# Cached attention on one core: the query weights of rounds 1 to 3 are loaded two head pairs at a time

## The chip, the core and the metric

The kernel runs on one core of a Trainium2 chip. TensorE multiplies matrices and writes to PSUM, eight banks of 2 KB a partition; VectorE and ScalarE copy out of PSUM and do the softmax; SyncE (SP) issues every load and store, which 16 DMA engines carry out; GpSimd does almost nothing here. The metric is the device time of one execution in microseconds. Three runs of the kernel before took 440.2, 445.95 and 443.5 us, so its median is 443.5 us.

## The reference: attention over a cache, with both projections

```python
B, Sq, D = 8, 112, 640
H, Sk, Dh = 32, 512, 192
q = (x @ wq).reshape(B, Sq, H, Dh).transpose(0, 2, 1, 3)
scores = einsum("bhqd,bhkd->bhqk", q, k_cache) * Dh ** -0.5
p = softmax(scores)
o = einsum("bhqk,bhkd->bhqd", p, v_cache)
out = o.transpose(0, 2, 1, 3).reshape(B, Sq, H * Dh) @ wo
```

All tensors are bf16. K and V have 8 x 32 x 512 x 192 elements each; wq is 640 x 6144, wo 6144 x 640.

## The kernel before

**Tiling.** The 32 heads go in four rounds of eight. In a round r, the kernel goes through the eight batches, and for each batch through two quads of four heads: 64 steps n in all, numbered in that order, two steps to a pair of round and batch i = n // 2. The queries of a round are made in two groups g = 2r and 2r + 1, four batches (448 rows) each. A group has four head pairs lp, and a head pair has 384 columns of wq, three blocks c of 128. So a fill Q(g, lp, c) is five matmuls over D = 640, each 128 weights by 448 rows, and evQ copies it out of PSUM.

**A step.** Sm and St make the scores of a step (with qc, copies of queries to the other half of the partitions, ahead of them); smax on VectorE scales them and takes the maximum, exp on ScalarE, rc and norm on VectorE divide by the sum; PT transposes p on TensorE and evPT copies it out; PVt and PVm multiply with V; evPV copies the result to oT. O multiplies oT with wo, and oacc adds that up over the rounds. For steps 57 to 61, p is transposed by a DMA (TD) instead of PT. exp of step n + 2 writes where p of step n lay, so it waits for PT or TD of step n.

**Loads.** K of a round and batch comes by a transposing DMA, (K, i), or plain, in halves of four heads, (KN, i, ...), and is then transposed on TensorE (KT). V comes in halves (V, i, half) of 768 KB. x comes in three loads X and is transposed on TensorE in seven chunks XT(c) of 128 rows, which evX copies out of PSUM.

**Query weights.** One SBUF tile wq_sb holds the weights of one round, four head pairs. (WQ, r, lp, n) loads n head pairs from lp on, 640 rows of n x 768 B (line 205): with n = 1 it is 480 KB, with n = 2, 960 KB. It overwrites weights of the round before, so for r > 0 it waits for all the fills of group 2r - 1 that read them, three for each head pair (line 207). Fills of the round wait for the load that brings their head pair (wq_piece, line 697). Each load has the semaphore of its first head pair.

**What sets the order.** Nothing is reordered at run time. ORDER_PE, ORDER_ACT, ORDER_DVE and ORDER_SP list the operations of each engine by hand; BANKS says which PSUM bank each result gets. An engine goes through its list, and for each operation waits for the semaphores of what it needs (lines 37 to 48); what stands behind a waiting operation waits too. An operation that writes a bank waits for the copies out of what lay in it before. On SP there is one rule more (lines 1105 to 1108): each load waits for an earlier load to land, the nearest one that has loads of a total size of at least 0.95 between it and this one. Sizes are in units of 1.5 MB: a V half is 0.5, a K of the transposing kind counts 1.5, a WQ load 1/3 for each head pair.

```python
            add("SP", ("WQ", r, lp, n), [q_done(2 * r - 1, lp + i, c) for i in range(n) for c in range(3)] if r else [],
                emit, f"mWQ{lp}", 16)
```

In round 0, head pairs 1 and 0 come as single loads and pairs 2 and 3 as one; in rounds 1 to 3 all four come one by one. Of the fills that they wait for, TensorE's list has Q(1, 1, 2) behind PT(2) and KT(3, 0); Q(1, 3, 0) behind KT(4, 0); Q(3, 1, 1) behind PT(19) and Q(3, 3, 2); Q(3, 3, 1) between the two halves of O(1, 4); Q(5, 1, 2) ahead of the scores of step 37, and Q(5, 3, 1) behind PT(37). Q(4, 0, 0), the first reader of round 2's weights, follows Q(3, 1, 1) with Q(3, 2, 2), PVt(18) and both PVm(18) between them.

**The start.** TensorE runs 18 matmuls on zeros, then XT 0, 1, 3, 2, then Q(0, 1, 1) and Q(0, 0, 0). XT(1) and XT(3) both have bank 4, so XT(3) waits for evX(1). evX 0, 3 and 2 are ScalarE's, evX 1 is VectorE's. Q(0, ...) reads all four chunks.

Of the kernel before, what the change touches and what calls it, by code (L numbers as in the profile page):

```python
# [52 lines left out]
def build_mha_kernel(nc, x, k_cache, v_cache, wq, wo, out):  # L53
# [33 lines left out]
    with ExitStack() as es:  # L87
# [145 lines left out]
        def pv_all(n):  # L233
# [108 lines left out]
            ('evX', 0), ('evX', 3), ('evX', 2), ('evQ', 0, 0, 0), ('evQ', 0, 0, 1), ('evK', 0, 1, 1), ('evK', 0, 1, 0),  # L342
# [73 lines left out]
            ('evX', 1), ('evQ', 0, 1, 1), ('evQ', 0, 1, 0), ('evK', 0, 0, 0), ('evX', 5), ('evK', 0, 0, 1), ('qc', 0),  # L416
            ('evQ', 0, 3, 1), ('smax', 0, 0), ('evK', 0, 3, 0), ('smax', 0, 1), ('smax', 0, 2), ('smax', 0, 3),
# [783 lines left out]
```

## Time and profile before

| | before |
|---|---|
| median of three runs | 443.5 us (440.2 to 445.95) |
| the profiled execution | 439.52 us |
| its span, first to last instruction | 437.5 us |
| TensorE busy (matmuls) | 420.4 us, 96% |
| VectorE busy | 375.2 us, 86% |
| ScalarE busy | 337.5 us, 77% |
| mean granted TensorE clock | 0.994 |
| bytes moved by DMA | 122.03 MB, mean 279 GB/s |
| loads of wq | 14 of 480 KB, median 6.2 us from issue to landing; 1 of 960 KB, 7.5 us |

The profile is of one execution. Its rows give a start in us from the beginning of the span, a duration, the engine (PE is TensorE, DVE VectorE, ACT ScalarE; SPq is SyncE's sequencer), the line of the kernel, the operation, what is written and read, and the number of instructions merged in the row; in square brackets the idle time of the engine before it and what ended it. On SPq, start and duration are those of the issue, not of the transfer; rows of the DMA view give KB and the us from an issue to its landing. The chain of waits is followed back from the last instruction; its rows have start, duration and what ran or was awaited. In the view by windows a row has the stretch and its length, then for PE, PEld, DVE, ACT and POOL the busy us and the number of instructions, then the granted clock, the share of the DMA engines that were busy, and GB/s.

### The profile page before, as it was taken

To read this page: it belongs to the slowest core of one execution; us is meant where nothing else is said; L and a number is where in the kernel's file an instruction comes from. 1 tells how busy PE (TensorE), PEld (TensorE's weight loads), DVE (VectorE), ACT (ScalarE), POOL (GpSimd) and SP (SyncE) were. 2 spreads that over 40 slices of the span, in tenths; PEclk is the share of its full clock that TensorE was granted. 3 is DMA by queue.
4 is the path that set the end of the run, shared out by engine and by line. 5 is a ranking of instruction groups with operands and counts; after the bars stand their busy time and mean duration, and the time that the engine had idled before them with its cause. 6 is when DMAs were issued, how large, how long until landed. Compare 5 with 4: busy or idle time off the path is not lost.

```text
span 437.5 us, 16223 instructions
## 1 busy us (share of the span) xinstructions
PE 420.4 (96%) x6805; PEld 290.6 (66%) x6805; DVE 375.2 (86%) x1198; ACT 337.5 (77%) x741; POOL 0.7 (0%) x6
## 2 busy tenths in 40 slices
PE   7999999899999999989999999999999999998986
PEld 4566667676766767657676666676667667665886
DVE  1399999889898899979899889989989889997971
ACT  3499999897978786778787668877878777866764
POOL 0000000000000000000000000000000000000000
PEclk9999999999999999999999999999999999999999
DMA  8999999999999999999999999999999999999963
GB/s 272 369 348 340 345 236 320 194 331 356 234 293 261 306 231 364 346 204 303 225 215 342 302 212 274 361 368 244 233 252 347 228 246 367 285 253 238 227 189 95
DMA packets 222857, 122.03 MB, mean 279 GB/s; under 512 B 165312, under 2 KB 222784, under 8 KB 222784
## 3 DMA queue, kind: packets, MB, share of 16 engines
q1 hardware_dynamic: 222784, 120.99, 109.7%
q8 instruction: 54, 0.88, 0.8%
q14 instruction: 19, 0.16, 0.1%
HBM read 78.22 MB, written 1.15 MB: 181 GB/s over the span
## 4 chain that ended last, share of the span: by engine, by line
PE 76%; DMA 10%; ACT 8%; DVE 4%; issue 2%; SPq 0%; ACTq 0%; DVEq 0%
PE ps L939 18%; PE ps L719 16%; PE ps L772 16%; PE ps L917 10%; PE ps L905 6%; PE ps L873 5%; ACT p_sb L834 4%; DMA vt<-in_v_cache_dram 3%; DMA kt<-in_k_cache_dram 2%; DVE s_sb L829 2%; ACT kt L146 2%; ACT qr L146 1%; DMA wq_sb<-in_wq_dram 1%; DMA qr<-p_sb 1%; PE ps L671 1%
## 5 line engine op out<-in xcount | busy, mean ns | idle before, releaser
L834 ACT ACTIVATE p_sb<-s_sb,nmx 112x512 bf16<-112x512 f32 x256 | 182.9, 718 | 43.9 <-DVE s_sb L829 38.9
L829 DVE TENSOR_SCALAR_CACHE_REDUCE s_sb<-ps 112x512 f32<-112x512 f32 x256 | 168.6, 684 | 19.1 <-PE ps L772 10.2
L719 PE MATMUL ps<-xT_sb,wq_sb 128*128 128x448 bf16 x480 | 103.1, 358 | 2.5 <-ACT xT_sb L146 1.2
L772 PE MATMUL ps<-kt,qr 128*128 128x256 bf16 (+1 forms) x512 | 95.0, 272 | 1.7 <-DVE s_sb L829 1.7
L939 PE MATMUL ps<-oT_sb,wo_sb 128*128 128x448 bf16 (+1 forms) x480 | 92.8, 341 | 0.0
L772 PE MATMUL ps<-kt,qh 128*128 128x256 bf16 (+1 forms) x512 | 87.8, 272 | 0.0
L838 DVE TENSOR_SCALAR p_sb<-p_sb,rinv 112x512 bf16<-112x512 bf16 x256 | 81.3, 347 | 1.4
L719 PEld LDWEIGHTS ps<-xT_sb,wq_sb 128*128 128x128 bf16 x480 | 43.1, 98 | 41.5 <-issue 4.1
L939 PEld LDWEIGHTS ps<-oT_sb,wo_sb 128*128 128x128 bf16 x480 | 44.5, 98 | 34.6 <-issue 0.6
L146 ACT ACTIVATE oT_sb<-ps 128x672 bf16<-128x672 f32 x64 | 46.4, 726 | 25.1 <-PE ps L917 24.7
L146 ACT ACTIVATE pT_sb<-ps 128x768 bf16<-128x768 bf16 (+1 forms) x58 | 51.9, 901 | 11.2 <-PE ps L873 10.9
L772 PEld LDWEIGHTS ps<-kt,qr 128*128 128x128 bf16 (+1 forms) x512 | 44.1, 96 | 22.0 <-issue 11.2
L917 PE MATMUL ps<-pT_sb,vt 128*128 128x112 bf16 x944 | 55.7, 213 | 0.7 <-issue 0.7
L917 PEld LDWEIGHTS ps<-pT_sb,vt 128*128 128x128 bf16 x944 | 47.8, 98 | 5.3 <-issue 0.8
L834 ACT ACTIVATION_READ_ACCUMULATOR p_sb<-s_sb,nmx 112x1 f32 x256 | 49.5, 193 | 0.0
L772 PEld LDWEIGHTS ps<-kt,qh 128*128 128x128 bf16 (+1 forms) x512 | 44.1, 96 | 6.4
L147 DVE COPY pT_sb<-ps 128x1024 bf16<-128x1024 bf16 (+1 forms) x60 | 36.8, 621 | 5.2 <-PE ps L873 5.1
L146 ACT ACTIVATE qr<-ps 128x448 bf16<-128x448 f32 x65 | 34.2, 538 | 8.1 <-PE ps L719 7.5
L873 PE MATMUL ps<-ident,p_sb 64*128 64x64 bf16 (+1 forms) x1888 | 37.3, 185 | 2.1 <-issue 1.7
L873 PEld LDWEIGHTS ps<-ident,p_sb 64*128 64x128 bf16 (+1 forms) x1888 | 33.2, 94 | 8.3 <-issue 3.4
L905 PE MATMUL ps<-pT_sb,vt 128*64 128x112 bf16 x944 | 33.0, 215 | 2.6 <-DMA vt<-in_v_cache_dram 1.4
L905 PEld LDWEIGHTS ps<-pT_sb,vt 128*64 128x64 bf16 x944 | 25.6, 109 | 13.2 <-issue 2.6
(56 smaller groups left out, 248.6 us busy)
## 6 DMA issues: line engine op xcount, KB each, us to landing
vt<-in_v_cache_dram SPq DMA_DIRECT2D x64, 768.0 KB, 6.8
wo_sb<-in_wo_dram SPq DMA_DIRECT2D x8, 960.0 KB, 7.6
wq_sb<-in_wq_dram SPq DMA_DIRECT2D x14, 480.0 KB, 6.2
wo_sb<-in_k_cache_dram SPq DMA_DIRECT2D x6, 768.0 KB, 6.8
accT<-in_k_cache_dram SPq DMA_DIRECT2D x4, 768.0 KB, 6.9
vt<-in_k_cache_dram SPq DMA_DIRECT2D x2, 768.0 KB, 8.2
kt<-in_k_cache_dram SPq DMA_DIRECT2D x2, 768.0 KB, 6.5
out_dram<-xT_sb SPq DMA_DIRECT2D x8, 140.0 KB, 2.5
```

The source lines that it names most:

```text
L146: return e.activation(dst, src, ACTF.Copy)
L147: return e.tensor_copy(dst, src)
L671: ends = [e.transpose(psb[:, bank + t, y * 64:(y + 1) * 64], kn[i][64 * t:64 * t + 64, 2 * p + u, c * 128:(c + 1) * 128], ident[64 * t:64 ...
L719: mm = e.matmul(ps[:, bank, 0:SG], w, v, start=(dc == 0), stop=(dc == DC - 1))
L772: return e.matmul(ps[:, 2 * j + odd, hs], q, ktb[j][lo:hi, :, blk, h * 128:(h + 1) * 128], start=first, stop=last, skip_group_check=True)
L829: return e.tensor_scalar(s_sb[:, a, :].rearrange("p (e c) -> p e c", e=2), ps[0:SQ, 2 * j:2 * j + 2, h * 256:(h + 1) * 256], -scale, None, ...
L834: return e.activation(p_sb[:, k, :], s_sb[:, a, :], ACTF.Exp, bias=nmx[:, k:k + 1], scale=-1.0, accum_out=rsum[:, k:k + 1])
L838: return e.tensor_scalar(p_sb[:, k, :], p_sb[:, k, :], rinv[:, k:k + 1], None, op0=ALU.mult)
L873: ends.append(e.transpose(psb[:, bank + t, i * w:(i + 1) * w], p_sb[lo:hi, (4 * n + k) % 8, q * 128:(q + 1) * 128], ident[lo:hi, lo:hi]))
L905: mm = e.matmul(ps[64 * h:64 * h + 64, b0 + j, SQ:2 * SQ], vtb[:, h0 + 2 * j + h, d0:d0 + 64], pT(j, h, q), start=(q == 0), stop=(q == 3))
L917: mm = e.matmul(ps[:, b0 + j, 2 * h * SQ:(2 * h + 1) * SQ], vtb[:, h0 + 2 * j + h, d0:d0 + 128], pT(j, h, q), start=(q == 0), stop=(q == 3))
L939: mm = e.matmul(ps[:, bank_of["O", g, m], 0:nc_], wo_sb[:, k, m * 128:(m + 1) * 128], oT_sb[:, g % 2, k, 0:nc_], start=(k == 0), stop=(k = ...
```

## The change

In rounds 1 to 3 the four single loads of wq become two loads of two head pairs, (WQ, r, 0, 2) and (WQ, r, 2, 2), whose runs are 1536 B instead of 768 B. Their places in SP's list change too: in round 1 they stand where head pairs 1 and 3 were; in round 2 the first moves from ahead of K 12 to ahead of K 13, the second stands between the halves of V 12; in round 3 the first stands behind K 22 and the second between the halves of V 19. The order of all other loads among themselves stays, and TensorE's list stays as it is. The rule of lines 1105 to 1108 counts two thirds for a double, so some loads near them wait for another load's landing than before.

In the transposes of x, XT(3) has bank 2 in place of bank 4, and evX(2) moves from ScalarE's list to VectorE's, behind evX(1).

```diff
--- before.py
+++ after.py
@@ -339,7 +339,7 @@
             ('OF', 4), ('O6', 0, 1), ('PVm', 62, 0), ('PVm', 62, 1), ('O6', 2, 1), ('PVm', 63, 0), ('PVm', 63, 1),
             ('OF', 5), ('OL', 0, 0), ('OL', 1, 0), ('OL', 0, 1), ('OL', 1, 1), ('OF', 6), ('OF', 7)]
         ORDER_ACT = [
-            ('evX', 0), ('evX', 3), ('evX', 2), ('evQ', 0, 0, 0), ('evQ', 0, 0, 1), ('evK', 0, 1, 1), ('evK', 0, 1, 0),
+            ('evX', 0), ('evX', 3), ('evQ', 0, 0, 0), ('evQ', 0, 0, 1), ('evK', 0, 1, 1), ('evK', 0, 1, 0),
             ('evQ', 0, 1, 2), ('evQ', 0, 0, 2), ('evX', 6), ('evX', 4), ('evQ', 0, 3, 0), ('exp', 0, 0), ('evQ', 0, 3, 2),
             ('evQ', 0, 2, 1), ('evK', 0, 2, 1), ('evK', 1, 1, 1), ('exp', 0, 3), ('evK', 1, 2, 1), ('evQ', 0, 2, 2),
             ('exp', 0, 1), ('evK', 2, 1, 1), ('exp', 0, 2), ('evK', 1, 3, 0), ('evK', 1, 3, 1), ('evQ', 1, 1, 0),
@@ -413,8 +413,8 @@
             ('exp', 63, 0), ('exp', 63, 1), ('exp', 63, 2), ('evPV', 61), ('exp', 63, 3), ('evPT', 63, 1), ('oout', 3),
             ('evPV', 62), ('evPV', 63), ('oout', 5), ('oout', 4), ('oout', 6), ('oout', 7)]
         ORDER_DVE = [
-            ('evX', 1), ('evQ', 0, 1, 1), ('evQ', 0, 1, 0), ('evK', 0, 0, 0), ('evX', 5), ('evK', 0, 0, 1), ('qc', 0),
-            ('evQ', 0, 3, 1), ('smax', 0, 0), ('evK', 0, 3, 0), ('smax', 0, 1), ('smax', 0, 2), ('smax', 0, 3),
+            ('evX', 1), ('evX', 2), ('evQ', 0, 1, 1), ('evQ', 0, 1, 0), ('evK', 0, 0, 0), ('evX', 5), ('evK', 0, 0, 1),
+            ('qc', 0), ('evQ', 0, 3, 1), ('smax', 0, 0), ('evK', 0, 3, 0), ('smax', 0, 1), ('smax', 0, 2), ('smax', 0, 3),
             ('evK', 0, 2, 0), ('evK', 0, 3, 1), ('evK', 1, 1, 0), ('evK', 1, 2, 0), ('evQ', 0, 2, 0), ('qc', 2), ('qc', 1),
             ('evK', 2, 1, 0), ('rc', 0, 0), ('evQ', 1, 0, 1), ('rc', 0, 1), ('smax', 1, 0), ('smax', 1, 1), ('norm', 0, 1),
             ('evK', 1, 0, 1), ('evK', 1, 0, 0), ('norm', 0, 0), ('evK', 2, 2, 1), ('smax', 1, 2), ('smax', 1, 3),
@@ -554,25 +554,24 @@
         ORDER_SP = [
             ('X', 0), ('X', 1), ('WQ', 0, 1, 1), ('WQ', 0, 0, 1), ('KN', 0, 0, 4), ('X', 2), ('WQ', 0, 2, 2),
             ('KN', 0, 4, 4), ('KN', 1, 0, 4), ('KN', 1, 4, 4), ('KN', 2, 0, 4), ('KN', 2, 4, 4), ('V', 2, 0), ('V', 2, 1),
-            ('V', 0, 0), ('V', 0, 1), ('KN', 3, 0, 4), ('WQ', 1, 0, 1), ('KN', 3, 4, 4), ('KN', 4, 0, 4), ('KN', 4, 4, 4),
-            ('V', 1, 0), ('V', 1, 1), ('V', 3, 0), ('V', 3, 1), ('WQ', 1, 1, 1), ('KN', 5, 0, 4), ('K', 6), ('WQ', 1, 3, 1),
-            ('KN', 5, 4, 4), ('WQ', 1, 2, 1), ('V', 4, 0), ('V', 4, 1), ('K', 7), ('K', 8), ('WO', 0, 1), ('WO', 0, 0),
-            ('V', 6, 0), ('V', 5, 0), ('V', 6, 1), ('V', 5, 1), ('V', 7, 1), ('V', 7, 0), ('K', 10), ('K', 9), ('V', 8, 1),
-            ('V', 8, 0), ('K', 11), ('V', 9, 1), ('V', 9, 0), ('WQ', 2, 0, 1), ('K', 12), ('V', 10, 1), ('V', 10, 0),
-            ('V', 11, 0), ('K', 13), ('V', 11, 1), ('KN', 14, 4, 4), ('KN', 14, 0, 4), ('WQ', 2, 1, 1), ('WQ', 2, 2, 1),
-            ('V', 12, 1), ('V', 12, 0), ('WO', 1, 0), ('WO', 1, 1), ('WQ', 2, 3, 1), ('V', 13, 1), ('K', 16), ('K', 15),
-            ('V', 14, 0), ('V', 14, 1), ('V', 13, 0), ('V', 15, 1), ('K', 17), ('K', 18), ('K', 19), ('V', 15, 0),
-            ('V', 16, 0), ('V', 16, 1), ('V', 17, 0), ('V', 17, 1), ('V', 18, 0), ('V', 18, 1), ('K', 21), ('K', 20),
-            ('K', 22), ('WQ', 3, 1, 1), ('WQ', 3, 0, 1), ('V', 20, 0), ('WQ', 3, 2, 1), ('V', 20, 1), ('V', 19, 0),
-            ('V', 19, 1), ('WQ', 3, 3, 1), ('WO', 2, 0), ('WO', 2, 1), ('V', 21, 0), ('V', 21, 1), ('V', 22, 0),
-            ('V', 22, 1), ('K', 23), ('K', 25), ('K', 24), ('K', 26), ('V', 24, 0), ('V', 24, 1), ('V', 23, 0),
-            ('V', 23, 1), ('V', 25, 0), ('V', 25, 1), ('K', 28), ('K', 27), ('K', 29), ('V', 27, 0), ('V', 27, 1),
-            ('V', 26, 0), ('V', 26, 1), ('WO', 3, 0), ('WO', 3, 1), ('V', 28, 0), ('V', 28, 1), ('K', 30), ('K', 31),
-            ('TD', 57), ('TD', 58), ('V', 29, 0), ('V', 29, 1), ('TD', 59), ('V', 30, 0), ('TD', 60), ('V', 30, 1),
-            ('TD', 61), ('V', 31, 1), ('OUT', 1), ('V', 31, 0), ('OUT', 3), ('OUT', 2), ('OUT', 0), ('OUT', 5), ('OUT', 4),
-            ('OUT', 6), ('OUT', 7)]
+            ('V', 0, 0), ('V', 0, 1), ('KN', 3, 0, 4), ('KN', 3, 4, 4), ('KN', 4, 0, 4), ('KN', 4, 4, 4), ('V', 1, 0),
+            ('V', 1, 1), ('V', 3, 0), ('V', 3, 1), ('WQ', 1, 0, 2), ('KN', 5, 0, 4), ('K', 6), ('WQ', 1, 2, 2),
+            ('KN', 5, 4, 4), ('V', 4, 0), ('V', 4, 1), ('K', 7), ('K', 8), ('WO', 0, 1), ('WO', 0, 0), ('V', 6, 0),
+            ('V', 5, 0), ('V', 6, 1), ('V', 5, 1), ('V', 7, 1), ('V', 7, 0), ('K', 10), ('K', 9), ('V', 8, 1), ('V', 8, 0),
+            ('K', 11), ('V', 9, 1), ('V', 9, 0), ('K', 12), ('V', 10, 1), ('V', 10, 0), ('V', 11, 0), ('WQ', 2, 0, 2),
+            ('K', 13), ('V', 11, 1), ('KN', 14, 4, 4), ('KN', 14, 0, 4), ('V', 12, 1), ('WQ', 2, 2, 2), ('V', 12, 0),
+            ('WO', 1, 0), ('WO', 1, 1), ('V', 13, 1), ('K', 16), ('K', 15), ('V', 14, 0), ('V', 14, 1), ('V', 13, 0),
+            ('V', 15, 1), ('K', 17), ('K', 18), ('K', 19), ('V', 15, 0), ('V', 16, 0), ('V', 16, 1), ('V', 17, 0),
+            ('V', 17, 1), ('V', 18, 0), ('V', 18, 1), ('K', 21), ('K', 20), ('K', 22), ('WQ', 3, 0, 2), ('V', 20, 0),
+            ('V', 20, 1), ('V', 19, 0), ('WQ', 3, 2, 2), ('V', 19, 1), ('WO', 2, 0), ('WO', 2, 1), ('V', 21, 0),
+            ('V', 21, 1), ('V', 22, 0), ('V', 22, 1), ('K', 23), ('K', 25), ('K', 24), ('K', 26), ('V', 24, 0),
+            ('V', 24, 1), ('V', 23, 0), ('V', 23, 1), ('V', 25, 0), ('V', 25, 1), ('K', 28), ('K', 27), ('K', 29),
+            ('V', 27, 0), ('V', 27, 1), ('V', 26, 0), ('V', 26, 1), ('WO', 3, 0), ('WO', 3, 1), ('V', 28, 0), ('V', 28, 1),
+            ('K', 30), ('K', 31), ('TD', 57), ('TD', 58), ('V', 29, 0), ('V', 29, 1), ('TD', 59), ('V', 30, 0), ('TD', 60),
+            ('V', 30, 1), ('TD', 61), ('V', 31, 1), ('OUT', 1), ('V', 31, 0), ('OUT', 3), ('OUT', 2), ('OUT', 0),
+            ('OUT', 5), ('OUT', 4), ('OUT', 6), ('OUT', 7)]
         BANKS = [
-            (('XT', 0), 5), (('XT', 1), 4), (('XT', 3), 4), (('XT', 2), 7), (('Q', 0, 1, 1), 6), (('Q', 0, 0, 0), 4),
+            (('XT', 0), 5), (('XT', 1), 4), (('XT', 3), 2), (('XT', 2), 7), (('Q', 0, 1, 1), 6), (('Q', 0, 0, 0), 4),
             (('Q', 0, 0, 1), 1), (('Q', 0, 1, 0), 7), (('KT', 0, 0), 0), (('KT', 0, 1), 5), (('Q', 0, 1, 2), 7),
             (('XT', 4), 2), (('Q', 0, 0, 2), 3), (('XT', 5), 6), (('XT', 6), 7), (('Q', 0, 3, 2), 6), (('Q', 0, 3, 1), 6),
             (('KT', 0, 3), 4), (('Q', 0, 3, 0), 4), (('Q', 0, 2, 0), 4), (('Q', 0, 2, 1), 4), (('KT', 0, 2), 0),
```

## The prediction, made before the change was run

> **What bounds the kernel now.** I read the page's busy shares first, then the order of time on SP (the engine that issues every load), then the times to landing, then the waits of TensorE.
>
> ```profile
> PE 420.4 (96%) x6805; PEld 290.6 (66%) x6805; DVE 375.2 (86%) x1198; ACT 337.5 (77%) x741; POOL 0.7 (0%) x6
> ...
> DMA  8999999999999999999999999999999999999963
> ```
>
> Two resources are full at once: TensorE (96%) and the DMA engines (90% or more in every slice from the second to the 38th). So a change that saves DMA time pays only where TensorE waits for a load, and one that stops TensorE or lets the DMA queue run dry can cost at once. TensorE's waits that end with a load or with what a load holds up are few; here they are, from the order of time on PE and ACT:
>
> ```profile
> 209.79 0.58 PE L905 MATMUL ps<-pT_sb,vt 128*64 128x112 bf16 x16 [0.69 <-DMA vt<-in_v_cache_dram]
> 284.43 0.58 PE L905 MATMUL ps<-pT_sb,vt 128*64 128x112 bf16 x16 [0.75 <-DMA vt<-in_v_cache_dram]
> 398.72 0.28 PE L772 MATMUL ps<-kt,qr 128*128 128x256 bf16 x1 [1.70 <-DVE s_sb L829]
> 397.12 0.72 ACT L834 ACTIVATE p_sb<-s_sb,nmx 112x512 bf16<-112x512 f32 x1 [2.03 <-DMA wq_sb<-p_sb]
> ```
>
> The last two belong together: the exponentials of step 59 wait 2.03 us for the DMA transpose of step 57 (its landing frees their place in p_sb), and through VectorE's maximum TensorE waits 1.70 us. That transpose stands in SP's queue behind the last two K transposes; the first row is SP's order of time, the second the chain of waits:
>
> ```profile
> 376.87 15.08 SPq L158 DMA_TRANSPOSE kt<-in_k_cache_dram  x2
> 392.05 4.99 DMA wq_sb<-p_sb
> ```
>
> SP is done with the K transposes at 376.87 + 15.08 = 391.95 and issues the transpose of p at 392.05. So the end is set by how far SP's queue has come at 392 us, and by TensorE where it is later than that. Those are the two delays that I follow.
>
> **The change part by part.** First the price of a load. A load's landing is its issue plus its time to landing, and in a full queue a load costs the time from the landing before it to its own. The rows are SP's order of time and, from the DMA view of short windows, the time to landing of the load issued there (the row with 6.34 is from the chain of waits, which has both in one):
>
> ```profile
> 4.60 0.37 SPq L179 DMA_DIRECT2D accT<-in_x_dram  x1
> 7.49 0.37 SPq L205 DMA_DIRECT2D wq_sb<-in_wq_dram  x1
> accT<-in_x_dram SPq DMA_DIRECT2D x1, 480.0 KB, 7.7
> wq_sb<-in_wq_dram SPq DMA_DIRECT2D x1, 960.0 KB, 7.5
> 268.67 0.53 SPq L167 DMA_DIRECT2D vt<-in_v_cache_dram  x1
> vt<-in_v_cache_dram SPq DMA_DIRECT2D x1, 768.0 KB, 7.3
> 271.11 6.34 DMA wq_sb<-in_wq_dram
> 55.13 8.05 SPq L158 DMA_TRANSPOSE kt<-in_k_cache_dram  x1
> kt<-in_k_cache_dram SPq DMA_TRANSPOSE x1, 11.6
> 63.28 0.52 SPq L205 DMA_DIRECT2D wq_sb<-in_wq_dram  x1
> wq_sb<-in_wq_dram SPq DMA_DIRECT2D x1, 480.0 KB, 4.7
> ```
>
> Round 0 already has a double load, with runs of 1536 B: x lands at 4.60 + 7.7 = 12.3, the double at 7.49 + 7.5 = 15.0, so it costs 2.7 us. A single costs 277.45 - 275.97 = 1.5 us (late) or 67.98 - 66.73 = 1.25 us (behind a K transpose). Two singles for one double change the queue by 2.7 - 3.0 = -0.3 us to 2.7 - 2.5 = +0.2 us. I take -0.2, nearer to the single that stands among plain loads as most do. Six doubles: -1.2 us of queue, between -1.8 and +1.2. The six issues of 0.37 us that SP loses are hidden by its waits for landings.
>
> [...]
>
> **Round 2 pays for it.** A double overwrites the weights of two pairs, so it waits for all their six fills of the round before. The first double of round 2 stands where the V load of 150 us stood, and waits for fill (3,1,1). Order of time on SP, times to landing of the loads of 135.32, 135.74, 149.96 (third of the three from 145.66) and 151.90, and TensorE (the last row is from the chain of waits):
>
> ```profile
> 135.32 0.37 SPq L205 DMA_DIRECT2D wq_sb<-in_wq_dram  x1
> 135.74 9.81 SPq L158 DMA_TRANSPOSE kt<-in_k_cache_dram  x1
> 145.66 4.67 SPq L167 DMA_DIRECT2D vt<-in_v_cache_dram  x3
> 151.90 8.71 SPq L158 DMA_TRANSPOSE kt<-in_k_cache_dram  x1
> wq_sb<-in_wq_dram SPq DMA_DIRECT2D x1, 480.0 KB, 6.9
> kt<-in_k_cache_dram SPq DMA_TRANSPOSE x1, 14.2
> vt<-in_v_cache_dram SPq DMA_DIRECT2D x1, 768.0 KB, 6.0
> kt<-in_k_cache_dram SPq DMA_TRANSPOSE x1, 12.3
> 153.19 3.04 PE L719 MATMUL ps<-xT_sb,wq_sb 128*128 128x448 bf16 x15
> 157.46 1.11 PE L719 MATMUL ps<-xT_sb,wq_sb 128*128 128x448 bf16 x5
> 181.80 1.44 PE ps L772 x16
> ```
>
> The row of 15 matmuls is three fills, (3,1,1) the second: it ends at about 153.19 + 2/3 x 3.04 = 155.2. The row at 157.46 is fill (4,0,0), the first that needs the new weights. Before, their load was issued at 135.32 and had 15 us to spare. After the change, SP can issue it at 155.2 at the earliest, 2.3 us ahead of its reader. By then the queue is empty: before, the V load of 149.96 landed at 156.0, and without the single ahead of it (1.5 us, and whatever round 1 saves) it lands at 153 to 154.5. How long a double takes in an empty queue no row shows. The nearest are these, the first load of the program and the first half of wo, issued just behind a K transpose:
>
> ```profile
> kt<-in_x_dram SPq DMA_DIRECT2D x1, 320.0 KB, 3.0
> wo_sb<-in_wo_dram SPq DMA_DIRECT2D x1, 960.0 KB, 5.9
> ```
>
> Below: 3.0 us and the other 640 KB at the double's pace, 640/960 x 2.7 = 1.8, together 4.8. Above: 5.9. The queue is empty, so I take 4.8. The weights land at 155.2 + 4.8 = 160.0, and **TensorE stands still for 160.0 - 157.5 = 2.5 us** (up to 3.6). Behind the waiting instruction on SP are K of step pair 13, V 11 and all later loads. K 13 landed at 151.90 + 12.3 = 164.2. After the change it follows the double by what K 12 took behind its single, (135.74 + 14.2) - (135.32 + 6.9) = 7.7: 167.7, 3.5 us late. Three singles that stood after it give 4.5 and one double takes 2.7: the queue is 1.7 us late at 190. K 13 is read first by the scores of step 26, the row at 181.80, so this delay meets TensorE only later, at 209.79.
>
> Round 1: the first double waits for fill (1,1,2), which ends about when SP comes to it; it and its fellow save 0.4, which the wait in round 2 swallows, since that is paced by TensorE. Round 3: both doubles come after their fills; they save 0.4 more, which leaves the queue +1.3 us at 300 and at 392. The second stands two V loads further back than its pair's single did. A V load costs 768/960 x 2.7 = 2.2 us, so the second lands at about 275.97 + 2 x 2.2 + 2.7 = 283.1, and its reader is the second of these two fills:
>
> ```profile
> 281.10 2.07 PE L719 MATMUL ps<-xT_sb,wq_sb 128*128 128x448 bf16 x10
> ```
>
> It begins at 282.1, so it waits 1.0 us; since the V loads behind come no later for that, the wait takes the place of the 0.75 us at 284.43.
>
> **The start.** Giving the transpose of x chunk 3 its own bank takes away its wait for a copy, and moving one copy from ScalarE to VectorE lets two go side by side (order of time, PE and ACT; then the stretches by window and the chain of waits):
>
> ```profile
> 6.81 0.72 PE L654 MATMUL ps<-ident,kt 128*128 128x128 bf16 x10 [0.68 <-DVE xT_sb L147]
> 8.73 0.54 PE L719 MATMUL ps<-xT_sb,wq_sb 128*128 128x448 bf16 x2 [1.20 <-ACT xT_sb L146]
> 7.29 1.30 ACT L146 ACTIVATE xT_sb<-ps 128x640 bf16<-128x640 bf16 x2 [0.91 <-PE ps L654]
> 6.00:9.40 3.40, 1.52 (x16) 0.99 (x15) 0.49 (x1) 1.68 (x3) 0.00 (x0) 1.00 1.05 365
> 9.40:12.80 3.40, 3.40 (x11) 1.32 (x9) 0.62 (x1) 0.54 (x1) 0.00 (x0) 0.50 1.06 372
> 8.73 5.63 PE ps L719 x20
> 330.92 3.89 PE ps L719 x20
> ```
>
> At most both waits go, 1.9 us; at least the second copy of ACT's row, 1.30/2 = 0.65. I take 0.7, since the second fill waits for weights of its own. That moves fill (3,1,1), its reader and the whole stall 0.7 us ahead, as long as loads allow.
>
> **The sum.** The queue's delay at 392 is +1.3 - 0.7 = +0.6 us. TensorE's is 2.5 - 0.7 = +1.8, of which the waits of 0.69 and 0.75 us take up part, since their loads are late too: +0.6 to +1.0 at 390. There TensorE has 1.70 us of wait to give, so the queue decides: +0.6 us, not more than 0.2%. The profiled execution took 439.5 us round its span of 437.5; it is 4 us below the median of 443.5, and I carry the difference over: **444.1 us**.
>
> **The rivals.** (1) Slower: the stall is not taken up. After the stretch 6.00 to 9.40, in which TensorE was busy 1.52 of 3.40 us, the granted clock was 0.50 for the next 3.4 us, and 20 matmuls that take 3.89 us at full clock (the chain's row) took 5.63, that is 1.7 more. A stall of 2.5 to 3.6 us leaves a stretch as thin. Then TensorE is 1.8 + 1.7 = 3.5 us late, up to 4.6, and with the queue at its worst (+1.2 for the loads, +1.1 for the landing) the end is 2.5 to 4.6 us later: 446 to 448. It decides from where TensorE's delay at 390 passes 1.7 us. Against it: idle times of 1.7 us elsewhere left the clock at 1.0. [...]
> (2) Faster: the start keeps its full clock, so TensorE gains 0.7 + 1.7 = 2.4 us, the stall comes that much earlier and the doubles save 1.8: the queue at 392 is at 1.3 - 2.4 - 0.6 = -1.7 us, 441.8. For it: the missing 1.9 us of waits lie just in the stretch before the slow one. Against it: TensorE would soon run up against the loads, whose engines are full from the second slice on.
> (3) The change doesn't do what it says: runs twice as long move no faster. Then the queue is 1.2 us later than forecast: 445.3.
>
> **How the numbers follow.** Chances: forecast 0.42, (1) 0.21, (2) 0.10, (3) 0.06. Those all lie within 2% (8.9 us), about what a measurement of this kernel can tell from no change: its three runs lie between 440.2 and 445.95. The remaining 0.21 is for what no row shows, 0.14 of it slower (a second wait of SP behind the late TensorE, since every later load stands behind it) and 0.07 faster. So faster 0.07, same 0.79, slower 0.14. The range reaches from (2) to the upper end of (1), with 1 to 2 us for the scatter of a median: 440 to 449.5.
>
> **What would show it.** Fill (4,0,0) begins after a wait of 2 to 3.6 us on the load of wq, at 159 to 161; SP's first load of round 2 is issued when TensorE ends three fills, and nothing lands for some 6 us before it; K 13 lands 2 to 4 us later; fill (0,1,1) begins before 8.1; the 1.70 us wait at 398.72 shrinks. Wrong would be: weights that land without a wait in round 2, a clock of 0.50 after 160, or loads behind the late ones that TensorE has to wait for after 290.

## The result and the profile after

| | before | after |
|---|---|---|
| median of 22 runs each | 440.86 us (436.96 to 446.62) | 442.86 us (438.59 to 447.12) |
| ratio, after to before | | 1.0109, 95% interval 1.008 to 1.0139 |
| ratio of the two medians | | 1.0045 |
| the profiled execution, its span | 439.52 us, 437.5 us | 445.6 us, 443.3 us |
| matmuls, busy and count | 420.4 us, 6805 | 421.7 us, 6805 |
| idle time of TensorE ahead of the fills | 2.5 us | 8.9 us |
| DMA packets of SP's queue | 222784 | 218848 |

In what follows, a double is a load of two head pairs of wq, and a single a load of one. The changed kernel is slower, by 2.0 us between the medians. That is within the 2% that count as no change, and the forecast of 444.1 us is 1.2 us above the new median. The ratio of 1.0109 leaves out disturbed runs of either kernel, which with this scatter takes more of the slow half from before; so I read the size as 0.5 to 1.1%. The profiled execution of the changed kernel is one of its slower ones, and what only this trace shows is marked below.

The page's groups, before and after, first the fills (busy, mean ns; idle time ahead of them and what ended most of it):

```profile
L719 PE MATMUL ps<-xT_sb,wq_sb 128*128 128x448 bf16 x480 | 103.1, 358 | 2.5 <-ACT xT_sb L146 1.2
```
```profile
PE 421.7 (95%) x6805; PEld 291.5 (66%) x6805; DVE 376.0 (85%) x1199; ACT 337.2 (76%) x740; POOL 0.7 (0%) x6
...
DMA  8999999999999989999999999999999999999963
...
L718 PE MATMUL ps<-xT_sb,wq_sb 128*128 128x448 bf16 x480 | 102.8, 355 | 8.9 <-DMA wq_sb<-in_wq_dram 7.1
```

Of the fills' idle time 7.1 us now end with a load of wq: 1.48 + 0.32 at the start, 2.95 in round 2, 2.38 in round 3. The 8 in the fifteenth slice of the DMA line, among the nines, is the empty queue of round 2. The chain of waits around it:

```profile
155.14 2.01 PE ps L718 x10
...
157.16 5.25 DMA wq_sb<-in_wq_dram
...
162.47 1.97 PE ps L718 x5
```

TensorE ends fill (3,1,1), SP issues the double at 157.16, it lands 5.25 us later, TensorE begins fill (4,0,0) 0.05 us after that. A load is on the path that sets the end, with its whole time. TensorE in order of time, and then the stretches by window (length; PE, PEld, DVE, ACT, POOL busy; granted clock, share of the DMA engines, GB/s):

```profile
162.47 1.97 PE L718 MATMUL ps<-xT_sb,wq_sb 128*128 128x448 bf16 x5 [2.95 <-DMA wq_sb<-in_wq_dram]
...
167.07 1.12 PE L718 MATMUL ps<-xT_sb,wq_sb 128*128 128x448 bf16 x5
```
```profile
155.75:159.17 3.42, 3.42 (x42) 1.95 (x40) 3.37 (x11) 2.08 (x5) 0.00 (x0) 1.00 0.26 26
159.17:162.58 3.41, 0.46 (x8) 0.29 (x6) 2.54 (x10) 2.55 (x7) 0.00 (x0) 1.00 1.07 334
162.58:165.99 3.41, 3.41 (x13) 1.62 (x11) 0.00 (x0) 0.00 (x0) 0.00 (x0) 0.50 1.28 290
```

From 155.75 to 159.17 the DMA engines are 26% busy: until 157.16 SP waits for TensorE. Then TensorE is busy for 0.46 us of 3.41, and in the 3.41 us after that its clock is granted at 0.50: the five matmuls of a fill take 1.97 us at 162.47 and 1.12 at 167.07. Fill (4,0,0) begins 5.0 us later than before (162.47 against 157.46; 1.9 of it had come earlier), and the scores of step 24, at 171.63 before, 6.68 us later.

In round 3 (first the chain of waits of before, then after: order of time on PE, and the chain):

```profile
277.47 6.83 DMA vt<-in_v_cache_dram
```
```profile
289.53 1.12 PE L718 MATMUL ps<-xT_sb,wq_sb 128*128 128x448 bf16 x5 [2.38 <-DMA wq_sb<-in_wq_dram]
290.58 0.58 PE L904 MATMUL ps<-pT_sb,vt 128*64 128x112 bf16 x16
291.72 0.58 PE L904 MATMUL ps<-pT_sb,vt 128*64 128x112 bf16 x16 [0.56 <-DMA vt<-in_v_cache_dram]
```
```profile
276.40 6.86 DMA vt<-in_v_cache_dram
...
283.28 8.31 DMA vt<-in_v_cache_dram
```

V 19,1 lands at 277.47 + 6.83 = 284.30 before and at 283.28 + 8.31 = 291.59 after, and PV of step 39 begins 0.13 us behind it in both (284.43, 291.72): that load sets the time here. The loads issued at 271.11 before and at 276.40 after go when K 22 lands. From there to the landing of V 19,1 before needs 284.30 - 271.11 = 13.2 us and after 291.59 - 276.40 = 15.2.

At the end (order of time on ACT and PE, then the chain):

```profile
403.19 0.72 ACT L833 ACTIVATE p_sb<-s_sb,nmx 112x512 bf16<-112x512 f32 x1 [1.73 <-DMA wq_sb<-p_sb]
404.80 0.28 PE L771 MATMUL ps<-kt,qr 128*128 128x256 bf16 x1 [1.39 <-DVE s_sb L828]
```
```profile
398.17 4.94 DMA wq_sb<-p_sb
```

The transpose of step 57 is issued 6.12 us later than before (398.17 against 392.05), and the matmul that waits through it 6.08 us. The waits there are still there, 0.3 us shorter each.

### The profile page after: what moved, and what is told of

Read it like the earlier page. It is cut to its first block, busy times and chain, and to the rows that moved or that the text cites. A ratio compares the mean times of both kernels' runs of the same rounds, so it can differ in the third digit from the quotient of the medians.

```text
span 443.3 us, 16208 instructions
## 1 busy us (share of the span) xinstructions
PE 421.7 (95%) x6805; PEld 291.5 (66%) x6805; DVE 376.0 (85%) x1199; ACT 337.2 (76%) x740; POOL 0.7 (0%) x6
## 2 busy tenths in 40 slices
DMA packets 218920, 122.01 MB, mean 275 GB/s; under 512 B 165216, under 2 KB 218848, under 8 KB 218848
## 3 DMA queue, kind: packets, MB, share of 16 engines
q1 hardware_dynamic: 218848, 120.99, 108.2%
## 4 chain that ended last, share of the span: by engine, by line
PE 75%; DMA 16%; DVE 5%; ACT 2%; issue 2%; SPq 0%; DVEq 0%; ACTq 0%
PE ps L938 17%; PE ps L771 17%; PE ps L718 15%; PE ps L916 11%; PE ps L904 6%; PE ps L872 6%; DMA vt<-in_v_cache_dram 5%; DMA wq_sb<-in_wq_dram 4%; DMA kt<-in_k_cache_dram 2%; PE ps L670 2%; DVE s_sb L828 2%; DMA wo_sb<-in_k_cache_dram 2%; DMA qr<-p_sb 1%; DMA wq_sb<-p_sb 1%; DVE p_sb L837 1%
## 5 line engine op out<-in xcount | busy, mean ns | idle before, releaser
L771 PE MATMUL ps<-kt,qr 128*128 128x256 bf16 (+1 forms) x512 | 96.0, 274 | 1.4 <-DVE s_sb L828 1.4
L771 PE MATMUL ps<-kt,qh 128*128 128x256 bf16 (+1 forms) x512 | 88.7, 274 | 0.0
L146 ACT ACTIVATE oT_sb<-ps 128x672 bf16<-128x672 f32 x64 | 46.4, 727 | 26.3 <-PE ps L916 25.9
```

What stands on the lines that cost most here:

```text
L146: return e.activation(dst, src, ACTF.Copy)
L771: return e.matmul(ps[:, 2 * j + odd, hs], q, ktb[j][lo:hi, :, blk, h * 128:(h + 1) * 128], start=first, stop=last, skip_group_check=True)
```

## The experiments

Executions of one kernel scatter by 4 us and more on either side, so one or two microseconds are read from traces; the times say what of it reaches the end. Batches were (e1 to e4), (e5, e9, e10, e7) and (e11, e12, e13), each with runs of the kernel before beside them.

| run | what differs | median (runs) | before beside it | ratio, 95% interval | wait at fill (4,0,0), half clock behind it |
|---|---|---|---|---|---|
| after | | 442.86 (22) | 440.86 | 1.0109 (1.008 to 1.0139) | 2.95, yes |
| e1 | round 2 single | 442.07 (6) | 439.88 | 1.0097 (1.0016 to 1.0178) | 0, no |
| e2 | only round 2 double | 442.69 (6) | 439.88 | 1.015 (1.0093 to 1.0207) | 3.00, yes |
| e4 | fill later | 441.59 (6) | 439.88 | 1.0131 (1.0066 to 1.0196) | 0.72, no |
| e7 | stall filled | 442.03 (12) | 441.60 | 0.9982 (0.9948 to 1.0016) | 0.38, no |
| e11 | stall half filled | 441.70 (12) | 441.29 | 1.0003 (0.9969 to 1.0038) | 1.75, no |
| e5 | second double of round 3 earlier | 445.16 (12) | 441.60 | 1.0061 (1.0007 to 1.0114) | 3.16, yes |
| e9 | V 20 behind V 19 | 444.92 (12) | 441.60 | 1.0023 (0.9985 to 1.006) | 3.03, no |
| e3 | only the start | 441.42 (6) | 439.88 | 1.0113 (1.0056 to 1.0171) | 0, no |
| e12 | all but the start | 445.06 (12) | 441.29 | 1.0067 (1.003 to 1.0104) | 3.16, yes |
| e10 | e1 with e9 | 441.49 (12) | 441.60 | 1.0072 (1.0007 to 1.0137) | 0, no |
| e13 | start, singles, V 20 later | 443.27 (12) | 441.29 | 1.0034 (0.9986 to 1.0081) | 0, no |

### The stall of round 2: there or not

e1 puts round 2's singles back into their places in the changed kernel; e2 makes round 2 alone double in the kernel before.

```diff
-  ('V', 9, 0), ('K', 12), ... ('V', 11, 0), ('WQ', 2, 0, 2), ('K', 13), ... ('V', 12, 1), ('WQ', 2, 2, 2),
+  ('V', 9, 0), ('WQ', 2, 0, 1), ('K', 12), ... ('K', 13), ... ('WQ', 2, 1, 1), ('WQ', 2, 2, 1), ('V', 12, 1), ... ('WQ', 2, 3, 1),
```

> The changed kernel with round 2's four single loads of wq in their old places; the doubles of rounds 1 and 3 and the change at the start stay. Theory A (the first double of round 2 waits for fill (3,1,1), TensorE stands 3 us for it and the slow clock that follows costs 1.7 more): no wait ahead of fill (4,0,0), granted clock 1.0 from 155 to 170, and 4 to 5 us less than the changed kernel, so a ratio to the kernel before of 0.997 to 1.002. The wait of 2.4 us in round 3 stays, about 1.5 of it more than before. Theory B (double loads as such, or the spacing of loads that counts them as two thirds, slow the queue): about a third of the loss goes, ratio 1.006 to 1.009.

> The kernel before with round 2's two double loads alone, in the places that the change gives them; start and rounds 1 and 3 as before. Theory A: TensorE waits 2.5 to 3.5 us ahead of fill (4,0,0), a stretch of 3.4 us at clock 0.50 follows, and the ratio is 1.007 to 1.012. Theory B: a third of the loss, ratio 1.003 to 1.005, with no wait of more than 1 us there.

Without the double TensorE goes from PV of step 18 to fill (4,0,0) without a wait (e1, order of time on PE); with it alone, in the kernel before, there is the wait and the half clock (e2, order of time on PE and windows):

```profile
155.54 0.96 PE L917 MATMUL ps<-pT_sb,vt 128*128 128x112 bf16 x16
156.33 1.11 PE L719 MATMUL ps<-xT_sb,wq_sb 128*128 128x448 bf16 x5
```
```profile
160.72 0.55 PE L719 MATMUL ps<-xT_sb,wq_sb 128*128 128x448 bf16 x1 [3.00 <-DMA wq_sb<-in_wq_dram]
```
```profile
156.85:160.26 3.41, 0.87 (x16) 0.71 (x16) 2.75 (x12) 2.84 (x7) 0.00 (x0) 1.00 0.90 298
160.26:163.67 3.41, 2.95 (x11) 1.53 (x12) 0.31 (x1) 0.00 (x0) 0.00 (x0) 0.50 1.26 284
```

The double of round 2 makes the stall, with or without the rest. The times of six runs, 442.07 and 442.69, don't separate. The ratios miss theory A: e1's 1.0097 is above even B's 1.006 to 1.009, e4's 1.0131, below, lies in B's range, and e2's 1.015 is above A's 1.007 to 1.012. But e3, below, has none of the new doubles and stands at 1.0113, where 0.997 to 1.000 was expected. So the times of this batch can't tell what the doubles cost; here the traces decide.

### The stall: the load or the idle engine

e4 moves the fill that waits, with its copy, behind PT(20) in the changed kernel. e7 and e11 leave it where it is and give TensorE 14 or 7 matmuls to do whose result nobody reads.

```diff
-  ('PVm', 18, 1), ('Q', 4, 0, 0), ... ('PT', 20),
+  ('PVm', 18, 1), ... ('PT', 20), ('Q', 4, 0, 0),
```
```diff
+  for i in range(14):
+      mm = e.matmul(ps[:, bank_of["Q", 4, 0, 0], 0:SG], ident[:, :], xT_sb[:, 0, 0:SG], start=True, stop=True)
```

> The changed kernel with fill (4,0,0) and its copy moved behind the scores and transposes of step 22 (PT 20), about 2.9 us later on TensorE; all loads as in the changed kernel. Theory A: the wait ahead of fill (4,0,0) falls from 2.95 us to under 0.5, no clock of 0.50 after it, 4 to 5 us less than the changed kernel, ratio to the kernel before 0.997 to 1.003, although SP still waits for fill (3,1,1) and K 13 is still late. Theory B: no gain, ratio 1.008 to 1.014.

> The changed kernel, with 14 more matmuls (448 rows each, their result is never read) on TensorE's list right ahead of fill (4,0,0), into the bank that this fill will overwrite: TensorE is busy for some 2.6 of the 2.95 us in which it waited for the weights of round 2. The weights land no sooner. Theory A (the half clock of 162.58 to 165.99 comes from the idle time of the stall): fill (4,0,0) begins at the same place, but the granted clock stays at 1.0 from 155 to 170, and TensorE is about 1.65 us further at 168 than in the changed kernel, counted from the start of that fill. Rival B (the half clock comes from something else, say from the work before or from the loads): it stays at 0.50 for 3.4 us behind fill (4,0,0).

> The changed kernel with 7 more matmuls of 448 rows ahead of fill (4,0,0) instead of the 14 of the run before: they fill some 1.3 of the 2.95 us, so that one idle stretch of about 1.65 us is left. The runs so far suggest a fixed grid of stretches of 3.41 us, each of which runs at half clock if TensorE was busy for less than about half (1.7 us) of the stretch before. Theory A (that rule): a single idle stretch of 1.65 us cannot make a stretch thinner than half, wherever it falls on the grid, so the granted clock stays at 1.0 from 155 to 170, and TensorE saves the 1.7 us of the half clock though it still stands for 1.5 to 1.9 us. Rival B (any idle stretch of over a microsecond can halve the clock): 0.50 for 3.4 us behind fill (4,0,0). If the stretch comes out above 1.71 us, either can happen and the run tells less.

e4, order of time on PE:

```profile
160.17 2.06 PE L729 MATMUL ps<-xT_sb,wq_sb 128*128 128x448 bf16 x10 [0.72 <-DMA wq_sb<-in_wq_dram]
...
211.92 0.39 PE L915 MATMUL ps<-pT_sb,vt 128*64 128x112 bf16 x8 [1.93 <-DMA vt<-in_v_cache_dram]
```

The wait falls to 0.72 us (expected: under 0.5), the clock stays whole, and TensorE, 0.7 us later than before at 171 us, loses 1.93 us at 211.92, where before lost 0.69: in the queue nothing landed for 6.8 us there too, and it is late by then. Moving the fill moves a part of the loss.

e7, order of time on PE and windows, then the same of e11:

```profile
155.86 2.81 PE L1038 MATMUL ps<-xT_sb,ident 128*128 128x448 bf16 x14
159.06 1.12 PE L722 MATMUL ps<-xT_sb,wq_sb 128*128 128x448 bf16 x5 [0.38 <-DMA wq_sb<-in_wq_dram]
```
```profile
155.75:159.16 3.41, 3.03 (x21) 1.50 (x19) 2.47 (x10) 2.48 (x7) 0.00 (x0) 1.00 1.08 341
159.16:162.57 3.41, 3.41 (x57) 2.30 (x57) 1.04 (x4) 0.65 (x2) 0.00 (x0) 1.00 1.27 290
```
```profile
155.97 1.49 PE L1038 MATMUL ps<-xT_sb,ident 128*128 128x448 bf16 x7
159.21 1.12 PE L722 MATMUL ps<-xT_sb,wq_sb 128*128 128x448 bf16 x5 [1.75 <-DMA wq_sb<-in_wq_dram]
```
```profile
155.61:159.02 3.41, 1.84 (x18) 0.94 (x15) 2.71 (x10) 2.72 (x7) 0.00 (x0) 1.00 1.01 324
159.02:162.43 3.41, 3.22 (x55) 2.30 (x56) 0.74 (x3) 0.54 (x1) 0.00 (x0) 1.00 1.28 290
```

In both the weights come no sooner, and the five matmuls of the fill take 1.12 us instead of 1.97: from there to the scores of step 24 e7 and e11 need 14.17 us and the changed kernel 15.84. Work that serves nothing saves the 1.67 us of the half clock. So theory A holds by the traces: the half clock comes from the idle stretch. The times point the same way, without proving it. The medians of e7 and e11 are 0.4 us above before's, the changed kernel's is 2.0 above. Over their runs the mean granted clock is 0.9965 and 0.9973, against 0.9933 in the changed kernel, and one half-clock stretch in 438 us makes 0.5 x 3.41 / 438 = 0.0039. But the kernel before has only 0.9942 and 0.9930 in these two batches, no clear difference from the changed kernel; by the traces it gets a half clock at its start instead. e11's 1.75 us are just above the 1.71 that its expectation set as the limit, so e11 alone would tell less.

### Round 3: a place or a sum

e5 issues the second double of round 3 two loads sooner, e9 moves the two loads of V 20 out of the way.

```diff
-  ('WQ', 3, 0, 2), ('V', 20, 0), ('V', 20, 1), ('V', 19, 0), ('WQ', 3, 2, 2), ('V', 19, 1),
+  ('WQ', 3, 0, 2), ('V', 20, 0), ('WQ', 3, 2, 2), ('V', 20, 1), ('V', 19, 0), ('V', 19, 1),
```
```diff
-  ('WQ', 3, 0, 2), ('V', 20, 0), ('V', 20, 1), ('V', 19, 0), ('WQ', 3, 2, 2), ('V', 19, 1),
+  ('WQ', 3, 0, 2), ('V', 19, 0), ('WQ', 3, 2, 2), ('V', 19, 1), ('V', 20, 0), ('V', 20, 1),
```

> The changed kernel, with round 3's second double, (WQ, 3, 2, 2), one place behind V 20,0 instead of behind V 19,0; nothing else. In the changed kernel fill (6,2,2) waited 2.38 us for it (287.15 to 289.53) and PV of step 39 another 0.56 us for V 19,1. Theory A: what holds TensorE here is the sum of the loads ahead of V 19,1 (the double brings the weights of head pair 3 ahead of it), not the double's place. Then the wait at fill (6,2,2) is gone (under 0.3 us), the wait ahead of PV of step 39 grows to 2.4 to 3.2 us, their sum stays within 0.6 us of 2.94, and the time is that of the changed kernel within 0.3%. Theory B: the place of the double is what costs; then the wait at PV of step 39 stays near 0.6, and TensorE and the time gain 2 us.

> The changed kernel, with both V 20 loads moved behind V 19,1, whose readers come 16 us later than those of V 19; the double stands between the halves of V 19 as before. Theory A (TensorE waits in round 3 because V 19,1 and the double stand behind 2 x 2.1 us of loads that nobody needs yet): the double and V 19,1 land about 4.2 us sooner after K 22 than in the changed kernel, neither fill (6,2,2) nor PV of step 39 waits (under 0.3 us together, 2.94 before), PV of steps 40 and 41 don't wait either, and TensorE is 2.5 to 3 us less late at 300 us. At the end part of it returns as a longer wait for the DMA transpose of step 57 (1.39 us in the changed kernel), since the queue is as late as before: the time is 0 to 2 us lower than the changed kernel's. Theory B (the queue is late by itself, whatever the order): a wait of the same sum at another place ahead of 300 us.

e5, then e9, both in order of time on PE:

```profile
283.70 2.06 PE L719 MATMUL ps<-xT_sb,wq_sb 128*128 128x448 bf16 x10
287.31 0.72 PE L905 MATMUL ps<-pT_sb,vt 128*64 128x112 bf16 x16 [1.55 <-DMA vt<-in_v_cache_dram]
289.45 0.36 PE L905 MATMUL ps<-pT_sb,vt 128*64 128x112 bf16 x7 [1.42 <-DVE p_sb L838]
```
```profile
283.83 1.04 PE L905 MATMUL ps<-pT_sb,vt 128*64 128x112 bf16 x32
...
400.80 0.40 PE L772 MATMUL ps<-kt,qr 128*128 128x256 bf16 x1 [4.24 <-DVE s_sb L829]
```

In e5 the fill waits no longer, and PV of steps 38 and 39 wait 1.55 + 1.42 = 2.97 us, where the changed kernel waited 2.38 + 0.56 = 2.94; theory A gave the sum, though part of it fell on V 19,0, one place before where I looked. (The last row names VectorE's p_sb, on which this PV doesn't depend; V 19,1, on which it does, landed at 289.31.) What holds TensorE in both is all that stands ahead of V 19,1. It does so only where the queue has no lead. In e1 and e7, whose list of loads in round 3 is the same, the load that goes when K 22 lands is issued at 270.62 and 267.89 (271.11 before, 276.40 in the changed kernel), and TensorE waits for no load of this stretch for more than 0.3 us; e1's expectation that the wait of 2.4 us stays was wrong.

In e9 both waits are gone: the two PV stand in one row. But the wait ahead of the end, 1.39 us in the changed kernel, is 4.24, so 2.85 of the 2.94 us came back there. A second loss follows it (e9, windows):

```profile
396.39:399.80 3.41, 0.17 (x2) 0.00 (x0) 0.00 (x0) 0.60 (x1) 0.00 (x0) 1.00 0.97 208
399.80:403.21 3.41, 2.41 (x24) 1.35 (x25) 3.09 (x11) 2.33 (x8) 0.00 (x0) 0.50 1.04 222
403.21:406.63 3.42, 3.42 (x27) 1.94 (x22) 3.19 (x12) 0.82 (x2) 0.00 (x0) 0.50 1.05 362
```

The wait empties a stretch, and the clock is 0.50 in the next two. From the issue of the transpose of step 57 to the end e9's trace needs 48.2 us, the twelve others 45.1 to 46.4. So its time does not show by itself that a wait in the middle is worth nothing, though it is that of e5 (444.92 and 445.16). Both are over 3 us above before beside them, the changed kernel 2.0: e5 was expected within 0.3% of the changed kernel, and e9 0 to 2 us under it. What e9's trace shows is where the wait went: SP issues that transpose at 394.09, 1.5 us earlier than in e5 but 2.0 later than before, and TensorE waits for it. The stretch of the stall in e9 tells something else, below.

### The start

e3 has the start alone; e12 all the doubles with the old start.

```diff
-  ('evX', 1), ('evQ', 0, 1, 1),
+  ('evX', 1), ('evX', 2), ('evQ', 0, 1, 1),
-  (('XT', 3), 4),
+  (('XT', 3), 2),
```

> The kernel before with the change at the start alone (bank 2 for the transpose of x chunk 3, one copy on VectorE); all loads of wq as before. If the start gained what the changed kernel's profile shows: fill (0,1,1) begins at 7.5 to 8.1, no clock of 0.50 before 13, and TensorE is 1.7 to 2.0 us ahead at 25 us. Theory A lets the queue of loads take most of it back (TensorE runs into loads): ratio 0.997 to 1.000. If TensorE alone set the time it would be 0.9955.

> The changed kernel with the start of the kernel before: XT(3) in bank 4, evX(2) on ScalarE; all doubles as in the changed kernel. Theory A (the start change is worth 0.3 to 0.9 us on TensorE, and in addition the 1.65 us of the half clock only where the old start happens to get it; by 75 us the loads have taken back all of it): TensorE reaches XT 5 at 14.2 to 16.4 us instead of 14.35, but fill (4,0,0) within 0.7 us of the changed kernel's 162.46, since it waits for the same double load, which waits for a fill that is itself held by loads; and the time is that of the changed kernel within 0.4%. Rival B (the gain at the start lives on to the end): 1 to 2.5 us slower than the changed kernel.

The start of e2 (the old one) in windows, then of the changed kernel the first fills in order of time and the windows:

```profile
6.00:9.40 3.40, 1.52 (x16) 0.96 (x15) 0.49 (x1) 1.68 (x3) 0.00 (x0) 1.00 1.03 352
9.40:12.80 3.40, 3.40 (x28) 1.66 (x28) 0.67 (x2) 1.09 (x2) 0.00 (x0) 1.00 1.06 376
```
```profile
7.98 1.12 PE L718 MATMUL ps<-xT_sb,wq_sb 128*128 128x448 bf16 x5 [1.48 <-DMA wq_sb<-in_wq_dram]
9.42 3.01 PE L718 MATMUL ps<-xT_sb,wq_sb 128*128 128x448 bf16 x15 [0.32 <-DMA wq_sb<-in_wq_dram]
```
```profile
6.00:9.40 3.40, 1.62 (x15) 0.73 (x11) 1.23 (x3) 0.98 (x2) 0.00 (x0) 1.00 1.04 358
9.40:12.80 3.40, 3.38 (x45) 1.83 (x47) 0.70 (x2) 1.09 (x2) 0.00 (x0) 1.00 1.03 352
```

The old start gets the half clock in two of three traces (before, e12) and not in e2, with the same 1.52 us of work between 6.00 and 9.40 as before. On the grid of the last section e2's stretch there is 6.66 to 10.07, with 2.02 us of work; before's is 5.98 to 9.39, with 1.54. Counted at the sixth transpose of x, TensorE is ahead of before by 1.65 us in e2 (old start, whole clock), and by 1.54 to 2.79, mean 2.2, in the ten traces with the new start, of which none has the half clock: so the change itself is worth about 0.5 us (0.2 of it because the first transposes begin at 4.71 on average in the ten and at 4.90 in e2), since the fills now wait for their weights, and the rest of the 1.9 us of the changed kernel is the clock. Little of either is left in the traces: at 147 us, the scores of step 20, the ten stand between 1.8 us ahead of before and 4.6 behind it, mean 0.0; e3 went from 2.5 us ahead at 20 us to 0.2 behind at 73. In e12 fill (4,0,0) begins at 162.15 against 162.47 in the changed kernel, as theory A had it. In time e12 is less clear: 445.06 against 441.29 for before in its batch, some 1.8 us more than the changed kernel was above its own, which is at the edge of what A allowed and inside rival B's 1 to 2.5 us. The mean clock over its runs, 0.9916 against 0.9933, is 0.7 us of that; the rest stays open, and with it whether a gain at the start lives on. e3's median of 441.42 is not under the 439.88 of before beside it; its profiled execution, 442.42 us, got two half-clock stretches elsewhere (at 49 and 76 us, behind gaps of the kind told of at the end).

### A version to beat both

e10 joins e1 and e9, e13 is the kernel before with the new start and V 20 behind (WQ, 3, 3, 1).

> The changed kernel with round 2's four single loads in their old places, and both V 20 loads behind V 19,1. Keeps the doubles of rounds 1 and 3 and the start. If the losses of the changed kernel are the stall of round 2 (2.95 us, and about 1.7 us of half clock behind it) and the waits of round 3 (2.94 us), and the start is a gain of 1.9 us, all losses are gone and the gain stays: no wait at fills (4,0,0) and (6,2,2) nor ahead of PV of step 39, granted clock 1.0 from 150 to 300, and a time of 436 to 440 us, 0.3 to 1% under the kernel before. If the start's gain is taken up by the loads, the time is that of the kernel before within 0.5%.

> The kernel before with the new start, all query weights as single loads, and in round 3 both V 20 loads moved behind (WQ, 3, 3, 1). The two parts of the work that need no double, as a version that could beat both kernels. Theory A (the waits of 0.75 us in round 3 and the start are not what sets the end): no wait at PV of step 39, TensorE 0.7 to 2.5 us earlier at 300 us than in the kernel before, and at the end a longer wait for the transpose of step 57; a time within 0.4% of the kernel before. Rival B (what TensorE gains lives on): 438 to 439.5 us, 0.5% under it.

In e10's trace the stall, the half clock and the waits of round 3 are gone, the clock is 1.000 throughout and the span 434.8 us, 2.7 under before. But that is one execution; the median, 441.49, is that of before beside it (441.60), as expected for a start whose gain the loads take up, and not 436 to 440. e13 removes the wait of round 3 as well, and its trace shows 2.37 us ahead of the end in place of 1.70; its median of 443.27 is not under before's either. Nothing here beats the kernel before.

## Why the prediction was right

**Right: the stall and where it comes from.** Forecast 2.5 us, up to 3.6: 2.95, and 3.00, 3.03, 3.16 and 3.16 in four other traces. The double was issued at the end of fill (3,1,1) (157.16, its reader 2.3 us behind as forecast) and landed 5.25 us later; forecast 4.8 in an empty queue, bounded by 5.9. From the end of the V load at 155.2 to 162.4 nothing landed, 7.2 us, forecast some 6. K 13 landed 3.55 us later, forecast 3.5, but that is luck: the double landed at 162.42 and not at 160.0 (TensorE had lost 1.9 us ahead of round 2), and K 13 followed 5.36 us behind it and not 7.7.

**Wrong: the clock behind it.** The step that failed is "Against it: idle times of 1.7 us elsewhere left the clock at 1.0", by which the half clock was a rival with 0.21 instead of part of the forecast. Its price of 1.7 us was right (1.67), and "a clock of 0.50 after 160" stands among the prediction's own signs of being wrong. Idle times of 1.73 us from 192.2 and of 1.70 from 397.0 in the kernel before did leave the clock at 1.0. But so did 3.03 us in e9, over two stretches with 1.79 and 2.01 us of work, while 2.95 us in the changed kernel, in a stretch with 0.46, did not; e7 and e11, with 3.03 and 1.84 us of work in theirs, kept 1.0. So in these cases the half clock goes with how thin a stretch is, not with the length of the idle time. Against before, TensorE loses 4.6 to 5.0 us between the scores of steps 20 and 24 in the four traces with this half clock (the changed kernel, e2, e5, e12), and 3.2 to 3.3 in these three. SP waits for TensorE, so the queue takes part of it over: V 13,1 lands 3.0 to 3.2 us later in the four and 1.5, 2.5 and 1.6 in e7, e9 and e11, counted from what TensorE was late at step 20. The queue term of the sum, 1.7 us late at 190, is about what e7 and e11 show, and leaves out the half clock.

**Wrong: round 3.** "Since the V loads behind come no later for that" failed. The double brings head pair 3 ahead of V 19,1, where its single had stood behind; the 15.2 us from K 22 to V 19,1 are 2.0 more than before. So 2.38 + 0.56 us of waits took the place of 0.75, not 1.0, and the 0.56 at 291.72 are a small case of another listed sign, loads that TensorE has to wait for after 290. About 1.1 of the 2.0 are two doubles for three singles (2.75 + 2.63 against 1.34 + 1.45 + 1.50); the other 0.9 is one V load that took 3.6 instead of 2.6, and such a late one stands in this stretch, at another load, in e5, e9 and e10 too, but not in e1. Its cause is open. So is what this mis-sizing cost in time: e9 takes the waits away and gets a half clock at the end.

**Right in size: the loads.** Between landings a double costs 2.34 to 2.75 us in rounds 1 and 3 of the changed kernel's trace, two singles 2.66 to 3.0 in that of before. I took -0.2 each; the rows allow 0 to -0.4. The packets' summed time on the engines did not fall: 109.7% of 437.5 us before and 108.2% of 443.3 after are both 480 us. Third rival or not, no time came of it.

**Right for the wrong reason: the start.** Forecast 0.7 from the order of the copies; about 0.5 by the traces, bounded by the weights' landing. Rival 2's whole clock came as well, but its 441.8 did not: by 147 us the mean of the ten traces is back at zero, taken by waits for loads (1.24 us at 40.1 in e3) and by gaps that I hadn't reckoned with.

**Right: the queue decides at the end,** by the 6.12 us of the transpose beside the 6.08 of the matmul, and by e9, where TensorE comes to step 58 half a microsecond ahead of before and waits 4.24 us. In e7 and e11 it does not: TensorE waits there for less than 0.3 us. But the sum was too small. The forecast was +0.6 us, the medians say +2.0, between the forecast and rival 1's 2.5 to 4.6. In the profiled pair it is 5.84 at the last matmuls, and that pair exaggerates: 1.9 us of it were there ahead of round 2, from a gap of 1.73 us at 80.60 and the half-clock stretch at 84.07 behind it, which no other trace has. Two errors offset each other in the time itself: the base of 443.5 was 2.6 us above the median of 22 runs, the change 1.4 under.

## What to carry to other kernels

Joining two loads joins their conditions: the merged load waits for the later of its two predecessors, and it carries the less urgent half ahead of whatever stood between; look for both before counting what longer runs save. A stall can have a second price behind it: here the granted clock was 0.50 behind TensorE's 2.95 us, for 1.67 us more, and in e7 and e11 14 or 7 matmuls whose result nobody reads saved that in the trace, though the weights came no sooner; such dummy work can be worth a try where the wait can't be removed. A wait removed in the middle can come back where another resource sets the end: in e9 2.85 of 2.94 us did, and the wait of 4.24 us there had that second price too, a clock of 0.50 for two stretches.

## What the hardware showed that I had not expected

**In these traces the half clock follows a thin stretch of a fixed grid.** A half clock is recorded for 3.41 us at a time, in the changed kernel from 84.07 and from 162.58, 23 such lengths apart, in e3 from 48.90 and from 76.21, eight apart. Laid out from these records, the 13 traces have 1646 stretches of 3.41 us whose next is not cut off by the end of the span. Of the 7 in which TensorE was busy for under 44% (the most 0.34, in e11 at 281.90) all 7 were followed by 0.50; of the 10 between 44% and 51%, 4; of the other 1629, 1: the stretch at 399.80 in e9, which ran at 0.50 itself and was busy for 71%. In e9 the grid cuts the stall of 3.03 us in two, and the clock stays at 1.00 behind it (windows):

```profile
154.04:157.46 3.42, 1.79 (x35) 1.24 (x32) 3.37 (x11) 2.27 (x6) 0.00 (x0) 1.00 0.81 217
157.46:160.87 3.41, 2.01 (x15) 1.28 (x17) 0.59 (x4) 0.57 (x2) 0.00 (x0) 1.00 1.24 302
160.87:164.28 3.41, 3.41 (x54) 2.13 (x55) 2.94 (x9) 2.56 (x5) 0.00 (x0) 1.00 1.19 252
```

**Some gaps of TensorE end behind packets of the instruction queue.** There are gaps of TensorE that nothing in the profile ends ("issue"). They differ in place and length from run to run: 1.73 us at 80.60 in the changed kernel, 2.50 at 73.76 in e3, 2.37 at 381.73 in e7; one between 191 and 199 us stands in 12 of the 13 traces. In the 13 traces there are 39 of over 0.5 us, and in all 39 TensorE went on 1.25 to 1.61 us after the end of a 16 KB packet of the instruction queue, of which there are 53 or 54 in a whole run. The DMA view counts the packet on the same 16 engines as the loads. For e3, the DMA view of the stretch from 73.6 to 75.1, and two windows:

```profile
DMA  9999999999798989889999897998969999799996
...
q8 instruction: 1, 0.02, 4.6%
```
```profile
72.80:76.21 3.41, 0.96 (x44) 0.79 (x35) 1.55 (x5) 2.07 (x5) 0.00 (x0) 1.00 1.10 367
76.21:79.62 3.41, 3.36 (x23) 1.59 (x24) 2.52 (x7) 1.51 (x3) 0.00 (x0) 0.50 1.23 157
```

The packet of 73.72 ended at 74.83, TensorE went on at 76.26. These gaps sum to 2.4 us in the trace of before, 5.0 in that of the changed kernel and 6.5 in e3's, and where one thins a stretch the half clock can come on top, as in these rows (0.96 us of work, then 0.50). This may be much of the scatter of a kernel's executions, but only times and clocks are on record for most of them: in e3 the three at a clock of 0.991 to 0.992 took 442.42 to 442.68 us, the three at 0.996 to 1.000 took 440.05 to 440.43. That TensorE had run out of instructions in these gaps is my guess from the packets' times; no row shows it. That the packets come late because the load queue is full was not tested.
